# A Fourier transform, a mixture of experts and a rational layer on one core: odd frequencies from two half sums, a wider feature transform, and a rearranged hand-over

## Chip, cores, metric

One core of a Trainium2 chip. The metric is device microseconds (us) from start to end of one launch, less is better. The kernel before takes 3660.11 us, the median of three runs from 3656.12 to 3660.86.

## The reference, cut to what matters

```python
X = np.fft.fft(x, axis=1)          # x: (8, 3072, 256), float32
X = np.fft.fft(X, axis=2)
x = X.real.reshape(24576, 256)
logits = x @ w_gate                # 8 experts, one per token
expert = np.argmax(logits, 1)
gate = softmax(logits)[expert]
h = np.maximum(x[e] @ w1[e], 0)    # for the tokens of expert e: 256 -> 1024 -> 256
out = gate * (h @ w2[e])
h = out @ w_in                     # 256 -> 2048
g = (a0 + a1*h + a2*h**2 + a3*h**3) / (1 + |b0||h| + |b1|h**2 + 1e-6)
return g @ w_out                   # 2048 -> 256
```

## The kernel before, in words

**Two parts.** The first part (lines 226 to 928) computes the transform, chooses experts and writes each token's row into a DRAM buffer `xs`, sorted by expert. The second part (from line 933) runs the experts over 103 blocks of 256 sorted tokens and the rational layer over 96 blocks of tokens. The change lies in the first part and in the hand-over to the second.

**Steps.** The first part runs 16 steps, two for each of 8 batches (`jh` 0 and 1, half of the frequencies each), and a 17th that only finishes. `tc.manual_schedule()` is on: each engine runs its instructions in the order in which the code emits them, and so does SP, which issues nearly all DMAs on one queue. The main loop (lines 711 to 816) is thus the hand-written order. Work of three steps is interleaved in it: the sequence transform of step s, the feature transform of step s-1, the sorting and writing out of step s-2.

- *Folds* (`fold_a`, `fold_b`, `fold_c`, lines 302 to 343), on DVE: rows and columns that share a cosine or sine up to sign are added and subtracted, for the next batch. `ee` holds what the even frequencies need, `oo` what the odd ones need.
- *Sequence transform* (`stage1`, line 428), on PE in float32: for each step four sums, i = 0 and 1 over 3 chunks of 128 rows (even frequencies), i = 2 and 3 over 6 chunks (odd ones), 384 frequencies wide, so 18 matmuls. ACT moves each from PSUM into a tile `u`, with a correction row as a bias (`evac`).
- *Feature transform* (`stage2`, line 445; `second`, line 634): three groups g = 0, 1, 2 of a step, each for two sets of 128 frequencies. A set takes three matmuls of 137 columns, one of them only 8 rows deep (`u128`, the contribution of feature 128, through `rb`). ACT copies one half to SBUF (`pp`), and six DVE operations form sums and differences: rows `y` for a frequency and its mirror, and logits `L`. A group with g = 1 uses both even and odd `u`.
- *Choice and place* (`gate_a`, `gate_rank`, `gate_b`, lines 472 to 541): DVE and small f16 matmuls give each token its slot; `norms` (line 491) squares all 12 row sets of a step on ACT.
- *Scatter* (line 550): twelve indirect DMAs on POOL for a step, 128 rows each, into `xs`.
- *Weights' split* (`job_*`, lines 564 to 610): one 1 MB weight matrix for a step. SP loads it, ACT squares it into a sum (`job_square`, last on ACT in a step), a matmul with ones sums over partitions (in `gate_rank`), DVE makes a power of two (`job_factor`), ACT scales it in place and copies it to f16 (`job_scale`, `job_split`), POOL subtracts for the low half (line 605), SP stores 1 MB to `ws` at the head of the next step, behind the load of the next matrix. Two buffers each.

**Hand-over** (lines 818 to 1009, 1291 to 1309). The last step's tokens are sorted in two portions. ACT's queue writes eight zero blocks (line 839); DVE computes the block tables; SP reads an expert number and loads the first two blocks' weights into `wslot` (`gather_first`), then the first token blocks (`load`, line 1052). `words` decodes the float64 weights `w_in` on DVE in 12 portions, part of them in the last step and the rest at line 913. Then come the scale `sx`, `pairs` and `transp`, and the first expert matmul (line 1092).

Tables for the transform lie in the two `wslot` buffers until the weights need them.

## Time and profile before

| quantity | value |
|---|---|
| median of three runs | 3660.11 us |
| the profiled execution's own time | 3654.46 us |
| its span in the profile | 3652.7 us |
| mean granted TensorE clock | 0.974 of full |

All rows below are from the one profiled execution. A float32 matmul shows as two records in them. Busy time of an engine within a stretch is the union of its instructions; "idle before" names what ended a wait.

### The profile page before, as it was taken

Reading aid. Unit: us, or ns where it says so; the run is one execution under the profiler, and the core shown is the slowest. Engines: PE = TensorE matmul, PEld = TensorE weight load, DVE = VectorE, ACT = ScalarE, POOL = GpSimd, SP = SyncE. Lnnn points to the kernel's source line nnn. Section 1 sums busy time; section 2 is a strip of 40 time slices with the busy share of each in tenths; the row PEclk is TensorE's granted clock in tenths of the full one; section 3 lists DMA queues with packets and bytes.
Section 4 is the critical chain, followed back from the end, with each engine's and each line's share of the span. In section 5 each row is a group of like instructions: output and inputs, shape, how many; then the busy total and the mean of one; then the engine's idle time right before and its main releaser. Section 6 shows DMA issues by size and latency. Waiting matters only on the chain.

```text
span 3652.7 us, 76237 instructions
## 1 busy us (share of the span) xinstructions
PE 3490.5 (96%) x30238; PEld 3020.3 (83%) x30238; DVE 3126.7 (86%) x3629; ACT 3166.4 (87%) x3985; POOL 2899.8 (79%) x2569
## 2 busy tenths in 40 slices
PE   6999568999999999999999999999999999999997
PEld 3655357888888888888888888888888888888885
DVE  6888674898888888889888888889888888888987
ACT  3666445999999999999999999999999999999997
POOL 3777655888888888888888888888888888888876
PEclk9989689999999999999999999999999999999998
DMA  6665531322222121322231112221231112212110
GB/s 258 212 231 197 197 113 39 88 44 45 45 62 66 43 43 43 91 42 45 45 85 45 42 45 65 68 43 43 68 68 42 42 42 75 57 45 43 43 33 18
DMA packets 342823, 270.17 MB, mean 74 GB/s; under 512 B 180382, under 2 KB 317606, under 8 KB 335152
## 3 DMA queue, kind: packets, MB, share of 16 engines
q1 hardware_dynamic: 309184, 183.21, 21.1%
q0 software_dynamic: 33024, 79.96, 6.4%
q8 instruction: 237, 3.88, 0.6%
q10 hardware_dynamic: 256, 2.11, 0.2%
q14 instruction: 122, 1.00, 0.2%
HBM read 329.07 MB, written 96.92 MB: 117 GB/s over the span
## 4 chain that ended last, share of the span: by engine, by line
PE 88%; DVE 5%; issue 3%; ACT 2%; DMA 1%; another core or an unknown queue 0%; POOL 0%; ACTq 0%; POOLq 0%; DVEq 0%; SPq 0%
PE po L1252 27%; PE h L1092 14%; PE h L1093 14%; PE h L1095 14%; PE py L1095 5%; PE py L1092 5%; PE py L1093 5%; PE ps L437 3%; PE pq L456 1%; PE pq L454 1%; ACT sq L495 0%; PE pq L453 0%; PE pu L422 0%; DVE h L1230 0%
## 5 line engine op out<-in xcount | busy, mean ns | idle before, releaser
L1092 PE MATMUL h<-yr,win 128*128 128x256 f16 x3072 | 757.6, 274 | 8.0 <-DMA yr<-ys 4.6
L1093 PE MATMUL h<-yr,win 128*128 128x256 f16 x3072 | 757.5, 274 | 0.0
L1252 PE MATMUL po<-wout,ghi 128*128 128x256 f16 x6144 | 735.5, 273 | 10.8 <-ACT ghi L1239 7.6
L1252 PEld LDWEIGHTS <-ghi 128*128 128x128 f16 x6144 | 594.2, 98 | 81.2 <-ACT ghi L1239 12.2
L1095 PE MATMUL h<-yr,win 128*128 128x256 f16 x3072 | 588.7, 273 | 0.0
L1228 ACT ACTIVATE h<-L,bnd 128x1024 f32<-128x1024 f32 x385 | 429.6, 1116 | 19.9 <-DVE u__48655 L1219 1.5
L1092 PE MATMUL h<-xt,wslot 128*128 128x256 f16 x1648 | 406.7, 274 | 4.3 <-DVE hlo L1118 3.5
L1093 PE MATMUL h<-xt,wslot 128*128 128x256 f16 x1648 | 406.7, 274 | 0.0
L1252 PE MATMUL po<-wout,glo 128*128 128x256 f16 x3072 | 398.8, 273 | 2.2 <-POOL glo L1240 2.2
L1092 PE MATMUL py<-hhi,wslot 128*128 128x256 f16 x1648 | 374.2, 274 | 2.6 <-ACT hhi L1112 2.6
L1093 PE MATMUL py<-hhi,wslot 128*128 128x256 f16 x1648 | 374.2, 274 | 0.0
L1093 PEld LDWEIGHTS <-wslot 128*128 128x128 f16 x3296 | 324.0, 98 | 46.4 <-issue 7.9
L1095 PEld LDWEIGHTS <-wslot 128*128 128x128 f16 x3296 | 324.0, 98 | 42.1 <-issue 3.4
L1092 PEld LDWEIGHTS <-wslot 128*128 128x128 f16 x3296 | 324.0, 98 | 38.7
L1092 PEld LDWEIGHTS <-win 128*128 128x128 f16 x3072 | 301.6, 98 | 44.8 <-DMA yr<-ys 4.9
L1252 PEld LDWEIGHTS <-glo 128*128 128x128 bf16 x3072 | 300.4, 98 | 38.5 <-POOL glo L1240 3.6
L1095 PEld LDWEIGHTS <-win 128*128 128x128 f16 x3072 | 301.7, 98 | 35.8
L1093 PEld LDWEIGHTS <-win 128*128 128x128 f16 x3072 | 301.6, 98 | 35.7
L1095 PE MATMUL h<-xt,wslot 128*128 128x256 f16 x1648 | 316.1, 274 | 0.0
L552 POOL DMA_INDIRECT xs<-y,sli x192 | 215.2, 1121 | 91.5 <-issue 49.6
L1118 DVE SCALAR_TENSOR_TENSOR hlo<-h,hhi 128x1024 f16<-128x1024 f32 x197 | 239.7, 1217 | 23.9 <-ACT hhi L1112 17.4
L1265 POOL DMA_INDIRECT out_dram<-o,id x192 | 198.8, 1036 | 55.0 <-issue 46.5
(4935 smaller groups left out, 9499.9 us busy)
## 6 DMA issues: line engine op xcount, KB each, us to landing
xr<-xs SPq DMA_DIRECT2D x103, 258.0 KB
ys<-yw SPq DMA_DIRECT2D x103, 256.0 KB
yr<-ys SPq DMA_DIRECT2D x96, 256.0 KB
xh<-x_l SPq DMA_DIRECT2D x14, 1536.0 KB
wf<-in_moe_w_dram SPq DMA_DIRECT2D x16, 1024.0 KB
ws<-wh SPq DMA_DIRECT2D x16, 1024.0 KB
wslot<-ws SPq DMA_DIRECT2D x4, 1024.0 KB
xh<-x_l SPq DMA_DIRECT2D x4, 768.0 KB
```

What stands on the lines that cost most here:

```text
L437: nc.tensor.matmul(ps[0:m, 0:n], lhsT=lhsT, rhs=mat[:, c, 0:n], start=c == 0, stop=c == nk - 1)
L454: nc.tensor.matmul(pq[:, k, 0:137], lhsT=u128[0:B, par, jg:jg + 128], rhs=rb[0:B], start=False, stop=True)
L456: nc.tensor.matmul(pq[:, k, 256:393], lhsT=uou[0:P - 1, js], rhs=rs[0:P - 1], start=True, stop=True)
L552: ins = nc.gpsimd.indirect_dma_start(out=xs, out_offset=bass.IndirectOffsetOnAxis(ap=sli[:, t0 + t:t0 + t + 1], axis=0), in_=y[:, t], in_o ...
L1092: nc.tensor.matmul(ps, lhsT=wa[i], rhs=xa[i], start=i == 0, stop=False)
L1093: nc.tensor.matmul(ps, lhsT=wb[i], rhs=xa[i], start=False, stop=False)
L1095: nc.tensor.matmul(ps, lhsT=wa[i], rhs=xb[i], start=False, stop=i == n - 1)
L1118: V.scalar_tensor_tensor(out=hlo[:, sl], in0=ps, scalar=0.0, in1=hhi[:, sl], op0=ALU.max, op1=ALU.subtract)
L1228: nc.scalar.activation(out=ps, in_=L, func=AF.Exp, scale=-1.0, bias=st["bnd", j][3])
L1252: nc.tensor.matmul(ps[:, q], lhsT=g[:, f - fs[0], q * P:(q + 1) * P], rhs=wout[:, h, 4 * u + f], start=g is ghi and u == 0 and f == 0 and ...
L1265: ins = nc.gpsimd.indirect_dma_start(out=out, out_offset=bass.IndirectOffsetOnAxis(ap=t[:, q:q + 1], axis=0), in_=o[:, q], in_offset=None, ...
```

## The change

- Rows are dealt to chunks by parity, so that the sum of an odd frequency f over even rows and that over odd rows serve both f and its mirror 1536 - f. `stage1_odd` computes both sums for 384 frequencies over 3 chunks each; ACT moves one, and DVE's `parts` adds and subtracts the other. It runs twice for a batch: i = 2 late in a step with `jh` 0, i = 3 at the head of the step with `jh` 1. One table `co` and one `so` remain of two each.
- Feature 128's row becomes row 127 of the odd `u` tile, brought there by a DMA on SP's queue from `u128` (1.5 KB, from one partition to one): one for each `stage1` with i = 1, two in `parts` for i = 3. With it the feature transform takes two matmuls of 273 columns into the finished rows; ACT makes two copies of 512 elements out of PSUM, and DVE copies the logits.
- `norms` squares half of the row sets. The sum of a weight matrix is taken later in the step. `job_hi` scales and rounds in one ACT operation; `job_lo` forms the low half on DVE.
- `fold_c` writes `oo` in three pieces instead of one.
- Hand-over: `words` runs in the 15th and 16th steps, all 12 portions; the first block's weights are loaded in the 16th step, as expert 0's (every expert counts at least one block); the zero blocks go through SP; the scale's logarithm and the first `split_scale` come earlier.

```diff
+        tabs["co"] = carve(0, 6 * NH).rearrange("p (c j) -> p c j", c=6)
+        tabs["so"] = carve(1, 6 * NH).rearrange("p (c j) -> p c j", c=6)
         for i in range(2):
-            tabs[f"co{i}"] = carve(i, 6 * NH).rearrange("p (c j) -> p c j", c=6)
...
+        NC = D + 1 + 2 * E
+        rc, rs = carve(1, NC), carve(1, NC)
...
-                en.tensor_tensor(out=eo[2 + k][:, 3 * h:3 * h + 3], in0=f[:, 0], in1=f[:, 1], op=minus)
+                oo = eo[2 + k]
+                en.tensor_tensor(out=oo[:, h::3], in0=f[:, 0, 0::2], in1=f[:, 1, 0::2], op=minus)
+                for q in range(2):
+                    r = slice(64 * q, 64 * q + 64)
+                    en.tensor_tensor(out=oo[64 * h:64 * h + 64, 2 + 3 * q], in0=f[r, 0, 1], in1=f[r, 1, 1], op=minus)
...
+        def edge_col_odd():
+
+            pu = [psA.tile([P, 512], F32, tag="s1", name="pu") for _ in range(2)]
+            for q in range(2):
+                for i, c in enumerate((2 * q, 3 + 2 * q, 6 + q)):
+                    nc.tensor.matmul(pu[q][0:B, 0:NH], lhsT=xc[:, 3, c], rhs=tabs["co"][:, 3 * q + i],
+                                     start=i == 0, stop=i == 2)
...
+            if i == 1:
+                nc.sync.dma_start(out=ut[127:128], in_=u128[b:b + 1, 0, jh * NH:jh * NH + NH])
+            U[2 * b + jh][i] = ut
...
+        def stage1_odd(b, eo, i):
+
+            mat = tabs[("co", "so")[i - 2]]
+            m = 130 - i if i == 2 else P - 1
+            ps = [psA.tile([P, 512], F32, tag="s1", name="ps2") for _ in range(2)]
+            for q in range(2):
+                for c in range(3 * q, 3 * q + 3):
+                    nc.tensor.matmul(ps[q][0:m, 0:NH], lhsT=eo[i][:, c], rhs=mat[:, c], start=c == 3 * q,
+                                     stop=c == 3 * q + 2)
+            up, um = [p2.tile([P, NH], F32, tag=f"u{i}{q}", name=f"u{i}{q}") for q in range(2)]
+            evac(um[0:m], ps[0][0:m, 0:NH], ODD[i], [fb[0:m, i, s_, b:b + 1] for s_ in range(2)])
+            U[2 * b][i], U[2 * b + 1][i] = up, um
+
+            def parts():
+                a, o = um[0:m], ps[1][0:m, 0:NH]
+                V.tensor_tensor(out=up[0:m], in0=a, in1=o, op=ALU.add)
+                if i == 2:
+                    V.tensor_tensor(out=a, in0=a, in1=o, op=ALU.subtract)
+                else:
+                    V.tensor_tensor(out=a, in0=o, in1=a, op=ALU.subtract)
+                    for q, t in enumerate((up, um)):
+                        nc.sync.dma_start(out=t[127:128], in_=u128[b:b + 1, 1, q * NH:q * NH + NH])
+
+            return parts
...
-                nc.tensor.matmul(pq[:, k, 0:137], lhsT=ueu[:, js], rhs=rc, start=True, stop=False)
-                nc.tensor.matmul(pq[:, k, 0:137], lhsT=u128[0:B, par, jg:jg + 128], rhs=rb[0:B],
-                                 start=False, stop=True)
-                nc.tensor.matmul(pq[:, k, 256:393], lhsT=uou[0:P - 1, js], rhs=rs[0:P - 1],
-                                 start=True, stop=True)
-            pp = gp.tile([P, 2, 137], F32, tag="pp", name="pp")
-            nc.scalar.activation(out=pp, in_=pq[:, :, 0:137], func=AF.Copy)
-            La, Lm = L[:, 4 * g:4 * g + 2], L[:, 4 * g + 2:4 * g + 4]
-            ya, ym = y[:, 0:2], y[:, 2:4]
-            V.tensor_tensor(out=La, in0=pp[:, :, 129:137], in1=pq[:, :, 385:393], op=ALU.subtract)
-            V.tensor_tensor(out=Lm, in0=pp[:, :, 129:137], in1=pq[:, :, 385:393], op=ALU.add)
-            V.tensor_tensor(out=ya[:, :, 0:129], in0=pp[:, :, 0:129], in1=pq[:, :, 256:385], op=ALU.subtract)
-            V.tensor_tensor(out=ym[:, :, 0:129], in0=pp[:, :, 0:129], in1=pq[:, :, 256:385], op=ALU.add)
-            V.tensor_tensor(out=ya[:, :, 255:128:-1], in0=pp[:, :, 1:128], in1=pq[:, :, 257:384], op=ALU.add)
-            V.tensor_tensor(out=ym[:, :, 255:128:-1], in0=pp[:, :, 1:128], in1=pq[:, :, 257:384], op=ALU.subtract)
+                nc.tensor.matmul(pq[:, k, 0:NC], lhsT=u[2 * par][:, js], rhs=rc, start=True, stop=False)
+                nc.tensor.matmul(pq[:, k, 0:NC], lhsT=u[2 * par + 1][:, js], rhs=rs, start=False, stop=True)
+            nc.scalar.activation(out=y[:, 0:2, 0:D], in_=pq[:, :, 0:D], func=AF.Copy)
+            V.tensor_copy(out=L[:, 4 * g:4 * g + 4].rearrange("p (t k) e -> p t k e", t=2),
+                          in_=pq[:, :, D + 1:NC].rearrange("p k (t e) -> p t k e", t=2))
+            nc.scalar.activation(out=y[:, 2:4, 0:D], in_=pq[:, :, D:0:-1], func=AF.Copy)
...
-        def job_scale(n):
+        def job_hi(n):
             e, which = jobs[n]
-            wf = J[n][0]
-            nc.scalar.activation(out=wf, in_=wf, func=AF.Copy, scale=(s1c, s2c)[which][:, e:e + 1])
-
-        def job_split(n, engine=nc.gpsimd):
             wf, wh, _ = J[n]
-            nc.scalar.activation(out=wh[:, 0], in_=wf, func=AF.Copy)
-            engine.tensor_tensor(out=wh[:, 1], in0=wf, in1=wh[:, 0], op=ALU.subtract)
+            nc.scalar.activation(out=wh[:, 0], in_=wf, func=AF.Copy, scale=(s1c, s2c)[which][:, e:e + 1])
+
+        def job_lo(n):
+            e, which = jobs[n]
+            wf, wh, _ = J[n]
+            V.scalar_tensor_tensor(out=wh[:, 1], in0=wf, scalar=(s1c, s2c)[which][:, e:e + 1], in1=wh[:, 0],
+                                   op0=ALU.mult, op1=ALU.subtract)
...
+                Y[s] = p2.tile([P, 12, DX], F32, tag="y", name="y", bufs=3)
...
+            norms(Y[s][:, 4 * g:4 * g + 2], NQ[s][:, 2 * g:2 * g + 2])
...
-                yield from decode(raw_in[q % 3], win32[q], mq_in[:, q:q + 1])
-                if q == 0:
-                    load_words(3, raw_in[0])
+                yield from decode(raw_in[q % 2 if q < 2 else 0], win32[q], mq_in[:, q:q + 1])
+                if q in (0, 2):
+                    load_words(2 + q // 2, raw_in[0])
...
+        load_t("so")
...
-        load_t("co1")
+        load_t("se1")
         if B > 1:
             load_x(1, 1)
-        load_t("so1")
...
-                raw_in.append(wp.tile([P, 2048], F32, tag="wf", name="raw_c")
-                              .rearrange("p (f w) -> p f w", w=2).bitcast(I32))
-                load_words(2, raw_in[2])
+                for h in range(2):
+                    c = slice(4096 * h, 4096 * h + 4096)
+                    nc.sync.dma_start(out=wslot[0][:, c], in_=ws[0:P, c])
             if on:
                 b, jh = steps[s]
-                if jh == 0 and fold:
-                    nxt = new_eo()
-                u = U[s] = {}
-                if s and jh == 0:
-                    batch_row(b)
-                stage1(b, jh, eo, 0, u)
+                if jh == 0:
+                    if fold:
+                        nxt = new_eo()
+                    U[s], U[s + 1] = {}, {}
+                    stage1(b, 0, eo, 0)
+                else:
+                    parts = stage1_odd(b, eo, 3)
             if s == 0:
-                stage1(b, jh, eo, 2, u)
+                odd0 = stage1_odd(b, eo, 2)
                 job_square(0)
                 edge_logits()
-                batch_row(0)
+                odd0()
             if 2 <= s < NS:
                 second_norm(s - 2, 2)
             if fold:
                 fold_a(b + 1, jh)
+            if parts:
+                parts()
...
+                pr = gate_rank(s - 2, 12)
+                send(*finish(s - 2))
...
-                stage1(b, jh, eo, 1, u)
+                stage1(b, jh, eo, 1 - jh)
...
+            if s == NS - 2:
+                words(3)
...
+                    job_sum(n, pr[:, 144:145], start=False, skip_group_check=True)
+                    job_factor(n, pr[:, 144:145])
+                job_hi(n)
...
-                stage1(b, jh, eo, 2 if s else 1, u)
+                if s and jh == 0:
+                    parts = stage1_odd(b, eo, 2)
+                else:
+                    stage1(b, jh, eo, 1)
             if fold:
                 fold_c(b + 1, jh, nxt)
+            if parts:
+                parts()
...
-                job_split(n, nc.gpsimd if s != NS - 2 else V)
-            if on:
-                stage1(b, jh, eo, 3, u)
+                job_lo(n)
+            if s == NS - 2:
+                words(3)
...
-            v = nc.scalar.value_load(runi[0:1, e:e + 1], min_val=e * R, max_val=e * R + NT)
-            ins_z.append(nc.scalar.dma_start(out=xs[ds(v, TB), :], in_=cst["c_z"]))
+            v = nc.sync.value_load(runi[0:1, e:e + 1], min_val=e * R, max_val=e * R + NT)
+            ins_z.append(nc.sync.dma_start(out=xs[ds(v, TB), :], in_=cst["c_z"]))
...
-        for h in range(2):
-            gather_first(0, h)
...
+        V.tensor_scalar(out=nx2, in0=nx2, scalar1=1e-14, scalar2=None, op0=ALU.max)
+        nc.scalar.activation(out=nx1, in_=nx2, func=AF.Ln)
+        nc.scalar.activation(out=nx1, in_=nx1, func=AF.Exp, scale=-0.5)
...
-    pairs(0, 0)
-    pairs(0, 1)
...
+    step(3)
+    pairs(0, 0)
+    pairs(0, 1)
```

## Rows read from the trace of the kernel before

**Rows 1.** Page: span, PE's total, two groups of part 5.
```profile
span 3652.7 us, 76237 instructions
...
PE 3490.5 (96%) x30238; PEld 3020.3 (83%) x30238; DVE 3126.7 (86%) x3629; ACT 3166.4 (87%) x3985; POOL 2899.8 (79%) x2569
...
L552 POOL DMA_INDIRECT xs<-y,sli x192 | 215.2, 1121 | 91.5 <-issue 49.6
L1118 DVE SCALAR_TENSOR_TENSOR hlo<-h,hhi 128x1024 f16<-128x1024 f32 x197 | 239.7, 1217 | 23.9 <-ACT hhi L1112 17.4
```

**Rows 2.** Stretches: busy us of PE, PEld, DVE, ACT, POOL; PEclk, DMA share, GB/s.
```profile
28.64:78.01 49.37, 46.67 (x161) 25.04 (x162) 24.84 (x62) 23.16 (x48) 4.08 (x1) 0.97 0.61 225
78.01:97.14 19.13, 19.13 (x99) 12.71 (x98) 18.70 (x53) 15.12 (x41) 11.22 (x6) 1.00 0.46 148
78.01:352.20 274.19, 257.24 (x1195) 167.05 (x1194) 238.58 (x679) 183.62 (x478) 209.41 (x152) 0.91 0.65 217
398.45:473.88 75.43, 20.65 (x112) 13.96 (x111) 54.40 (x166) 19.98 (x61) 35.12 (x30) 0.56 0.51 173
```

**Rows 3.** PE in order of time: start, length, line, tiles, shape, records.
```profile
82.13 0.46 PE L503 MATMUL pr<-o,tri 128*128 128x88 f16 x11
...
83.02 2.18 PE L437 MATMUL ps<-se,ee 128*127 128x384 f32 x6
...
87.22 4.04 PE L437 MATMUL ps<-wslot,oo 128*128 128x384 f32 x12
91.09 0.40 PE L453 MATMUL pq<-wslot,u 128*128 128x137 f32 x2
...
473.88 0.37 PE L1092 MATMUL h<-xt,wslot 128*128 128x256 f16 x1 [0.78 <-DVE xt L1082]
```

**Rows 4.** DVE in order of time, two stretches.
```profile
211.13 0.17 DVE L462 TENSOR_TENSOR L<-pp,pq 128x16 f32<-128x16 f32 x1
...
212.62 0.25 DVE L476 TENSOR_REDUCE mx<-L 128x12 f32<-128x96 f32 x1
...
214.49 1.73 DVE L315 TENSOR_TENSOR fo<-xh 128x1524 f32<-128x1524 f32 x1
...
221.58 4.07 DVE L525 TENSOR_TENSOR pos<-pos,o 128x96 f32<-128x96 f32 x1
...
375.58 2.29 DVE L605 TENSOR_TENSOR wh<-wf,wh 128x2048 f16<-128x2048 f32 x1 [0.85 <-DMA xh<-in_moe_w_in_dram]
```

**Rows 5.** POOL in order of time; in brackets idle time and its releaser.
```profile
214.48 2.59 POOL L552 DMA_INDIRECT xs<-y,sli  x1 [0.30 <-issue]
...
221.43 4.09 POOL L605 TENSOR_TENSOR wh<-wf,wh 128x2048 f16<-128x2048 f32 x1
227.46 0.99 POOL L552 DMA_INDIRECT xs<-y,sli  x1 [1.94 <-DVE y L540]
...
375.73 3.00 POOL L552 DMA_INDIRECT xs<-y,sli  x1 [0.30 <-issue]
...
436.56 0.97 POOL L552 DMA_INDIRECT xs<-y,sli  x1 [6.22 <-DVE mx L476]
...
451.75 1.89 POOL L552 DMA_INDIRECT xs<-y,sli  x1 [0.30 <-issue]
```

**Rows 6.** SP (DMA issues) in order of time, two stretches.
```profile
201.79 0.38 SPq L569 DMA_DIRECT2D wf<-in_moe_w_dram  x1
202.22 0.46 SPq L609 DMA_DIRECT2D ws<-wh  x1
...
461.34 1.59 SPq L1052 DMA_DIRECT2D xr<-xs  x2
```

**Rows 7.** ACT in order of time, two stretches.
```profile
213.96 1.91 ACT L579 ACTIVATE wh<-wf 128x2048 f16<-128x2048 f32 x1 [2.05 <-issue]
...
432.57 0.40 ACT L459 ACTIVATE pp<-pq 128x274 f32<-128x274 f32 x1 [12.06 <-remote]
```

**Rows 8.** Chain of waits, first piece: start, length, what.
```profile
0.74 1.90 DMA pro<-x_r
```

274 lines of the change are left out of this document (131 added, 143 removed).

## Prediction

> **What bounds it now.** I read the stretches first, then the engines in order of time within one step. The second part of the kernel is PE at full clock and is left alone; the change must earn its time before 473.88 [rows 3]. The long piece there is the twelve steps from 78.01 to 352.20: 274.19 us, so 22.85 a step [rows 2]. PE is busy 257.24 of them, 94%, but at a granted clock of 0.91; the one step at clock 1.00, from 78.01 to 97.14, takes 19.13. So PE alone would need 19.13 / 0.91 = 21.0, and something else sets 22.85. POOL does: a scatter is 1.121 on the mean [rows 1] plus 0.30 between two [rows 5], twelve of them 17.05; then the subtraction of line 605, 4.09; then an idle 1.94 until DVE's `gate_b` has the next slots [rows 5]. The round is 23.1, the period within 1%. The reader is to see how it locks itself: DVE's line 525, in `gate_b`, lasts 4.07 and ends at 225.65 [rows 4], just after POOL's subtraction, which runs from 221.43 to 225.52. An operation of the same 96 elements takes 0.25 [rows 4]. DVE stands still for 3.8 us behind POOL, and POOL then waits for DVE. DVE is busy 238.58 / 12 = 19.9 a step, ACT 15.3, the DMA engines 0.65 x 22.85 = 14.9 [rows 2].
>
> **PE.** Six matmuls of 384 columns take 3.87 [rows 3], 0.645 each. Before: 18 x 0.645 = 11.6, ranks and sum 0.89 [rows 3], so 6.63 of the 19.13 for three feature groups, 2.2 each. After: 12 x 0.645 = 7.74; twelve matmuls of 273 columns at 273/384 of 0.645, 5.5 (1.84 a group); 0.89. Sum 14.1, or 15.5 at clock 0.91: 5.0 less at full clock, and off the bound if POOL or DVE keeps a longer round.
>
> **POOL.** The subtraction and its wait go; 17.05 of scatters stay. The new risk is `job_lo`: when DVE did one such subtraction (375.58, 2.29 long [rows 4]), the scatter begun at 375.73 lasted 3.00, against 0.99 and 0.97 at 227.46 and 436.56 [rows 5]; so did another lengthen, to 2.59 at 214.48, beside line 315's 1.73 [rows 4, 5]. The rounded ends are 0 and +2.0 a step, 17.05 to 19.1. I take 2.0: same data, same size, though `job_lo` is another operation. The Trainium skill (SBUF — State Buffer, "Who interferes with whom") says that a DVE instruction with two SBUF inputs contends with a GpSimd instruction that reads SBUF; by it the round is 19.1, without it 17.05, and the 3.00 agrees.
>
> **DVE.** Out go three groups' sums and differences, 1.49 each (211.13 to 212.62 [rows 4]), 4.5, and the collisions with line 605, up to 3.8. In come three logit copies at 0.17 as line 462 [rows 4], 0.5; `parts`, two operations of 384 elements, priced by line 1118 (1.217 for 1024 [rows 1]) at 0.46 each, 0.9; four more pieces in `fold_c`, 0.25 each at most, 1.0; `job_lo`, 2 x 1.217 = 2.4. From 19.9 that gives 20.2 less 0 to 3.8: 16.4 to 20.2. I take 17.6, since most steps collide. ACT gains six copies of 512 elements, a quarter of line 579's 1.91 [rows 7] plus overhead, 0.6 each, 3.6, and loses one pass of 2048, 1.9, and half the norms: at most 17.0, not the bound. DMA bytes hardly change.
>
> **The new wait.** In a step with `jh` 1 the second feature group reads the odd tile of i = 3, whose row 127 comes by a DMA that SP issues behind that step's weight load and store. Those two wait for `job_lo` of the step before, DVE's last act there: after PE's last group one logit copy 0.17, `gate_a` 1.9 (212.62 to 214.49 [rows 4]), `job_lo` 2.4, so 4.5 after PE has begun the new step; with two issues (0.43 and 0.46 [rows 6]) the rows leave at 5.4. No row shows a 1.5 KB transfer behind 2 MB. Ends: 1.9, as 32 KB took on an empty queue [rows 8], and 11.7, from the store's issue at 202.22 [rows 6] to 213.96, when `job_square`, which waits for load and store, began [rows 7]. I take 11.7: same queue, right behind the same transfers. So they land at 17.1 (at least 7.3). PE wants them after i = 3 (3.87), group 0 (1.84), the ranks (0.6) and i = 0 (1.94): 8.25, at clock 0.91 9.1. PE waits 8.0, and then has group 1, the sum, i = 1 and group 2, 5.9 or 6.5 at 0.91. That step takes 9.1 + 8.0 + 6.5 = 23.6; one with `jh` 0, where nothing fetched is read within the step, 15.5; the pair 39.1, **19.6 a step**. Behind PE in these 8 us wait ACT's copies, DVE's last logit copy, `gate_a` and `job_lo`, and so the next load: the wait feeds itself once a batch. POOL at 19.1 and DVE at 17.6 fit beneath. [...]
>
> **Twelve steps:** 12 x (22.85 - 19.6) = 39 less.
>
> **First two steps,** 28.64 to 78.01, 49.37 with PE busy 46.67 [rows 2]. Eighteen matmuls go (six in the first, twelve in the second, the edge columns included): 11.6 at most; nothing, if the second step already waits for its rows behind the first matrix's store. I take 6. Two tables less to load speak for more, but PE has no wait for them to lose.
>
> **15th and 16th steps.** All twelve decode portions now lie here, where folds are absent on DVE; the last one needs a load into a buffer that the previous portion frees, 1.9 to 11.7 of waiting on DVE, with the last slots behind it. Moving `job_lo` to DVE adds, dropping the sums takes away. I take 0, ends 6 better and 6 worse.
>
> **Hand-over.** ACT waited 12.06 at 432.57 to write `pp` [rows 7]; POOL then stood 6.22 before the last portion's scatters [rows 5]. `pp` is gone and a whole step's row tile was freed a step earlier: 6.2, at least 0. The last scatter ended at 451.75 + 1.89 = 453.64 [rows 5]; with 1.9 to land, 455.5, but the token load left at 461.34 [rows 6], behind the decodes: 5.8, at least 0. From there 12.5 passed to the first expert matmul [rows 3]; with the scale ready, I estimate 7.5 for load, split and transposes: 5, at least 0. Sum 17. The zero blocks on SP cost nothing while POOL still issues the last twelve scatters, 12 x 1.28 = 15 us: two issues with a register take 1.59 [rows 6], eight 6.4. Weights of block 0 come earlier and are off the path; the earlier `split_scale` hides behind the token load.
>
> **Sum.** 39 + 6 + 0 + 17 = 62. The profiled execution has a span of 3652.7 [rows 1] and its own time of 3654.46; less 62, **3592 us**. That execution is 5.6 below the median of the runs, which I leave within the range. About 0.2% is what a measurement of this kernel can tell from no change.
>
> **Rivals.** *Rows in time* (27%): the small DMAs land in 1.9 and `job_lo` does not stretch scatters. Then POOL at 17.05 and DVE at 17.6 set about 17.5: 12 x 5.35 = 64, start 11.6, tail 17, together 93: 3562. For it: their bytes are nothing. Against: the queue's order. *DMA in the way* (13%): 14.9 of DMA work a step is 76% of 19.6; the two weight transfers stretch from 11.7, ACT waits at `job_square`, PE at the sum. At 22 a step: 10 + 0 + 17 = 27: 3627. For it: the DMA share is 0.65 already. Against: a quarter of the DMA engines' time would still be free. *PE's clock falls* (6%), the slower side: PE, less busy, is granted the lower level of 1.2 GHz through the steps. Then its 14.1 take 28.3, longer than everything else: 12 x 5.4 = 65 more, less the tail's 17, 48 slower: 3702. For it: from 398.45 to 473.88 PE was busy 27% and its clock 0.56 [rows 2]. Against: PE would still be busy some 80%, nearer to the 94% that had 0.91. It decides where the clock falls below 14.1 / (22.85 + 17/12) = 0.58. *No gain* (4%): the 15th and 16th steps give back the tail's 17 and the rounds stay near 22: within 0.2%.
>
> **Numbers.** My forecast has 50%. Faster by over 0.2%: 0.50 + 0.27 + 0.13 and a little of the rest, 0.91; same 0.03; slower 0.06. The range: the low end is the first rival's 3562, less 6 for the 15th and 16th steps, 5 for steps at POOL's 17.05 and 6 for a shorter hand-over, 3545; the high end takes in the second rival's 3627, with 6 for those two steps and 3 for the hand-over, 3636.
>
> **What would show it.** Right: steps alternate, long with `jh` 1, PE idle before the second group until a DMA into `u`; scatters back to back on POOL, some near 3 us beside `job_lo`; line 525's successor at 0.25; first expert matmul some 62 earlier. Wrong: even steps of 17 to 18 with no such wait; ACT waiting for `ws` at `job_square`; a clock under 0.6 in the steps; DVE standing at a decode while POOL is idle in the 16th step.

## The result, and the profile after

The changed kernel takes 3627.52 us (median of four runs, 3622.71 to 3630.88) where the kernel before takes 3659.82 (3656.12 to 3660.86) on the same chip: ratio 0.9913, 95% interval 0.9895 to 0.993, 32 us less. The forecast, 3592, is 62 below the kernel before's profiled execution of 3654.46. The profiled execution has its own time of 3622.71 and a span of 3620.9.

The top of the page, to be held against [rows 1]: PE has 88 us less work, DVE 35, ACT 54, POOL 57, and the span is 32 shorter. What came off the engines did not all come off the time.

```profile
span 3620.9 us, 75124 instructions
...
PE 3402.7 (94%) x29842; PEld 2967.4 (82%) x29842; DVE 3091.3 (85%) x3424; ACT 3111.9 (86%) x3791; POOL 2842.4 (78%) x2558
```

To compare stages I need the same places in both. A pair of steps (one batch) begins with the six even matmuls of 385 columns. By these, the 3rd step of the kernel before begins at 78.01 and its 15th at 347.86; the 352.20 at which [rows 2] cut the stretch is 4.3 us into the 15th. The stretches of busy time (columns as in [rows 2]), first of the kernel before, cut there:

```profile
78.01:347.86 269.85, 252.90 (x1178) 164.21 (x1176) 234.28 (x665) 182.10 (x475) 206.06 (x148) 0.91 0.65 215
```

and of the changed kernel: first two steps, twelve steps, 15th and 16th to the first scatter of the 15th step's tokens, and from there to the first expert matmul.

```profile
29.32:74.17 44.85, 37.33 (x112) 19.68 (x113) 25.27 (x51) 16.91 (x31) 0.00 (x0) 0.92 0.46 166
74.17:323.83 249.66, 195.19 (x889) 130.04 (x887) 202.75 (x526) 142.63 (x329) 165.93 (x139) 0.87 0.74 243
323.83:398.64 74.81, 39.72 (x185) 25.59 (x185) 49.57 (x121) 32.64 (x75) 32.09 (x30) 0.76 0.53 191
398.64:449.62 50.98, 9.62 (x61) 6.37 (x60) 26.42 (x107) 7.83 (x24) 27.35 (x27) 0.60 0.45 141
```

| stage | before | after | gained | forecast |
|---|---|---|---|---|
| first two steps | 49.37 | 44.85, begun 0.7 later | 3.8 | 6 |
| twelve steps | 269.85 | 249.66 | 20.2 | 39 |
| 15th and 16th steps | 66.09 | 74.81 | -8.7 | 0 |
| hand-over | 59.93 | 50.98 | 8.9 | 17 |
| second part | 3178.8 | 3171.3 | 7.5 | 0 |

In the twelve steps no engine is full: PE 195 of 250 us at a granted clock of 0.87, DVE 203, POOL 166, the DMA engines 0.74. PE's list of waits in them (waited for: total, times, longest) has one large entry under two names. The wait is the same in all six batches; where the profile found no event for it, it says "issue".

```profile
PE pq L499 <- issue: 22.9, 3, 8.1
PE pq L499 <- DMA u<-u: 21.0, 3, 8.0
PE pr L544 <- issue: 4.1, 7, 0.9
PE pr L539 <- DVE o L522: 2.7, 3, 1.2
```

One step with `jh` 1, PE in order of time (216.20 to 241.23), then SP in the same step:

```profile
216.20 4.03 PE L474 MATMUL ps<-wslot,oo 128*127 128x384 f32 x12
...
222.57 2.18 PE L457 MATMUL ps<-wslot,ee 128*128 128x384 f32 x6
...
234.15 1.25 PE L499 MATMUL pq<-wslot,u 128*128 128x273 f32 x2 [8.01 <-issue]
...
235.48 4.07 PE L457 MATMUL ps<-se,ee 128*127 128x384 f32 x6
```

```profile
222.82 0.38 SPq L605 DMA_DIRECT2D wf<-in_moe_w_dram  x1
223.25 0.46 SPq L646 DMA_DIRECT2D ws<-wh  x1
223.76 1.17 SPq L488 DMA_DIRECT2D u<-u  x2
```

SP issues the 1 MB weight load, the 1 MB store and then the rows of 1.5 KB; PE goes on 10.4 us after the rows' issue began (10.1 to 10.5 in the six batches). Ahead of the load SP stood 6.1 us for `job_lo` of the step before (line 641), so the rows leave 7.6 us into the step. A row moves as 16 packets of 96 bytes; these start at 231.47, when those of the store are nearly out, the last one of the two rows ends some 8.7 us after the issue began, and the DMA engines are busy all that time. SP's wait, and the stretch from the issue on:

```profile
SPq L605 <- DVE wh L641: 6.1, 1, 6.1
```

```profile
223.76:232.69 8.93, 2.38 (x10) 1.38 (x8) 6.05 (x18) 1.89 (x6) 6.95 (x7) 0.80 1.00 326
235.48:239.55 4.07, 4.07 (x8) 2.33 (x9) 3.37 (x10) 2.96 (x7) 3.16 (x3) 0.53 0.21 76
```

Behind the wait stands a second cost: the six matmuls at 235.48 take 4.07, six of the same size at 222.57 take 2.18. PE had stood still for 8 us; in the 4 us of these matmuls its granted clock is 0.53 (second row), nearly all of it at the lower of its two levels (1.2 GHz), and they run at about half pace.

DVE and POOL, for the rounds of [rows 4, 5]: line 558, the successor of line 525, takes 0.25 where that took 4.07, and POOL has no subtraction, but the scatter that runs beside `job_lo` (line 641) lengthens.

```profile
203.79 2.34 DVE L641 SCALAR_TENSOR_TENSOR wh<-wf,s2c,wh 128x2048 f16<-128x2048 f32 x1
...
209.96 0.25 DVE L558 TENSOR_TENSOR pos<-pos,o 128x96 f32<-128x96 f32 x1
```

```profile
202.84 1.01 POOL L588 DMA_INDIRECT xs<-y,sli  x1 [0.30 <-ACT y L503]
204.16 2.83 POOL L588 DMA_INDIRECT xs<-y,sli  x1 [0.30 <-issue]
212.71 1.65 POOL L588 DMA_INDIRECT xs<-y,sli  x1 [5.72 <-issue]
```

In the 15th step the loads of `w_in`'s words, issued on SP at 332.50 behind 2 MB of weights, hold DVE at the first decode until 345.45. ACT's part of that decode stands ahead of its copies, so PE waits 9.61 next, and POOL runs dry for 17.05 (at 369.28) and 12.66 (at 398.64).

```profile
345.45 0.80 DVE L223 TENSOR_SCALAR xh<-xh 128x1024 int32<-128x1024 int32 x1 [7.36 <-issue]
```

```profile
354.70 1.65 PE L474 MATMUL ps<-wslot,oo 128*127 128x384 f32 x2 [9.61 <-ACT u L421]
```

In the hand-over POOL is no longer late (its longest idle is 2.20, against 6.22 in [rows 5]). But the last scatter ends at 433.4 and the first token load leaves at 442.98: the eight zero blocks on SP, which wait for DVE's counts, are issued from 423.09 to 440.02, and the load's last wait is for one of them to land. SP's waits (waited for: total, times, longest) and SP in order of time:

```profile
SPq L1096 <- DMA xs<-c_z: 1.6, 2, 1.4
```

```profile
423.09 16.93 SPq L878 DMA_DIRECT2D xs<-c_z  x8
442.98 1.64 SPq L1096 DMA_DIRECT2D xr<-xs  x2
```

### The profile page after: what moved, and what is told of

The parts are those of the page before. It is cut to its first block, busy times and chain, and to the rows that moved or that the text cites. A ratio compares the mean times of both kernels' runs of the same rounds, so it can differ in the third digit from the quotient of the medians.

```text
span 3620.9 us, 75124 instructions
## 1 busy us (share of the span) xinstructions
PE 3402.7 (94%) x29842; PEld 2967.4 (82%) x29842; DVE 3091.3 (85%) x3424; ACT 3111.9 (86%) x3791; POOL 2842.4 (78%) x2558
## 4 chain that ended last, share of the span: by engine, by line
PE 84%; DVE 7%; issue 3%; DMA 3%; ACT 2%; POOL 1%; SPq 0%; another core or an unknown queue 0%; POOLq 0%; DVEq 0%; ACTq 0%
PE po L1296 27%; PE h L1136 14%; PE h L1137 14%; PE h L1139 14%; PE py L1139 5%; PE py L1136 5%; PE py L1137 5%; PE ps L457 1%; DMA u<-u 1%; PE ps L474 1%; DMA xh<-in_moe_w_in_dram 0%; DVE wh L641 0%; PE pq L499 0%; DVE oo L352 0%; DVE h L1274 0%
## 5 line engine op out<-in xcount | busy, mean ns | idle before, releaser
L588 POOL DMA_INDIRECT xs<-y,sli x192 | 222.6, 1159 | 181.0 <-issue 102.8
```

The lines of the kernel that those rows point to most:

```text
L588: ins = nc.gpsimd.indirect_dma_start(out=xs, out_offset=bass.IndirectOffsetOnAxis(ap=sli[:, t0 + t:t0 + t + 1], axis=0), in_=y[:, t], in_o ...
```

## The experiments

Twelve kernels ran, in three groups of four, each group on one chip beside the kernel before (the second and the third group on the same chip). That kernel took 3642.4, 3645.5 and 3661.8 us in the three groups, so kernels are compared by their ratio to it, and stages only roughly across groups. The table is read like the one above; the clock is that granted to PE in the twelve steps.

| kernel | ratio to before (95%) | first two | a step | clock | 15th, 16th | hand-over |
|---|---|---|---|---|---|---|
| before, profiled first | 1 | 49.4 | 22.49 | 0.91 | 66.1 | 59.9 |
| changed, profiled first | 0.9913 (0.9895, 0.993) | 44.9 | 20.81 | 0.87 | 74.8 | 51.0 |
| changed, again | 0.9921 (0.9905, 0.9938) | 45.7 | 21.00 | 0.88 | 73.1 | 42.3 |
| rows on ACT's queue | 0.9844 (0.9827, 0.986) | 38.2 | 18.82 | 0.92 | 75.7 | 42.5 |
| rows early | 0.9827 (0.981, 0.9843) | 46.2 | 17.73 | 0.98 | 76.1 | 42.1 |
| weights after rows | 0.9799 (0.9775, 0.9823) | 39.0 | 18.42 | 0.95 | 70.6 | 48.6 |
| words first | 0.99 (0.9884, 0.9917) | 45.8 | 20.85 | 0.89 | 63.6 | 42.1 |
| rows and words | 0.9772 (0.9756, 0.9789) | 40.8 | 17.74 | 0.98 | 60.2 | 42.1 |
| before, with the new split | 0.9884 (0.9867, 0.99) | 50.2 | 19.40 | 0.99 | 51.6 | 56.0 |
| changed, with the old split | 1.0101 (1.0079, 1.0122) | 46.8 | 25.90 | 0.82 | 80.4 | 56.6 |

**Rows on ACT's queue.** The same transfers, issued by another engine.

```diff
-                nc.sync.dma_start(out=ut[127:128], in_=u128[b:b + 1, 0, jh * NH:jh * NH + NH])
+                nc.scalar.dma_start(out=ut[127:128], in_=u128[b:b + 1, 0, jh * NH:jh * NH + NH])
...
-                        nc.sync.dma_start(out=t[127:128], in_=u128[b:b + 1, 1, q * NH:q * NH + NH])
+                        nc.scalar.dma_start(out=t[127:128], in_=u128[b:b + 1, 1, q * NH:q * NH + NH])
```

> All the row transfers into the odd tiles are issued on ACT's queue instead of SP's, at the same place of the program. Theory (ring order: in the changed kernel PE's 8 us before the second feature group of each step with jh 1 is a 1.5 KB row standing behind the 2 MB that SP issued just before it): the row lands some 2 us after its issue, the 6.4 to 8.1 us idle of PE before line 499 goes, those steps fall from 25.0 to 17 to 18 us, and the kernel is 40 to 55 us shorter than the changed one, near 3575 to 3587. Rival 1 (the DMA engines are full with 2 MB whatever queue a transfer is in): the row lands as late as before, PE's idle stays, 3620 to 3630. Rival 2 (the wait is hidden behind another bound, DVE or POOL with the stretched scatters): PE's wait goes, but the steps fall by 2 to 3 us only, 3605 to 3615.

It gained some 27 us (0.9844 against 0.9917, the mean of the two runs of the changed kernel), about half of what the theory said. The trace shows why. SP issues the weights at 204.32 and 204.75; ACT issues the first row at 205.00, as soon behind the store as SP did; PE goes on at 212.30, 7.3 us after the issue began (6.5 to 7.3 in the six batches), not 10.4 and not 2. ACT's first issue and PE's wait in order of time, then PE's waits at this line in the twelve steps:

```profile
205.00 0.50 ACTq L488 DMA_DIRECT2D u<-u  x1
```

```profile
212.30 1.25 PE L499 MATMUL pq<-wslot,u 128*128 128x273 f32 x2 [4.69 <-DMA u<-u]
```

```profile
PE pq L499 <- DMA u<-u: 18.5, 5, 4.8
PE pq L499 <- DVE nrm L584: 8.6, 2, 4.5
```

So the place in SP's queue is worth 3 us of the 10.4. On a queue of its own the row's first packet still starts only 4.9 us after its issue (205.00) and the last ends after 7.0, where two rows with no other issue of SP in the 12 us before them (those of the first batch in the run of rows and words below, issued at 46.94) were through after 2.1. Theory and first rival each hold a part; whether it is the work of the DMA engines or the making of the packets that holds the row for the 4.9, no run separates. PE's wait at line 499 in the twelve steps is 27.1 us in all (the 8.6 put down to DVE are the wait of two batches at the same place), against 51.3 in the changed kernel run again.

**Rows early.** The two rows of the odd tiles go out at the start of the step before, ahead of that step's weights, from the second batch on.

```diff
-            up, um = [p2.tile([P, NH], F32, tag=f"u{i}{q}", name=f"u{i}{q}") for q in range(2)]
+            up, um = early.pop((b, i), None) or odd_tiles(i)
...
+            if on and s and s % 2 == 0:
+                early[steps[s][0], 3] = odd_tiles(3)
+                odd_rows(steps[s][0], early[steps[s][0], 3])
             for n in new:
                 job_load(n)
```

> The two rows of the odd tiles of i = 3 are fetched at the start of the step before, ahead of its weight load on SP, from the second batch on; nothing else changes queue. Theory (order on SP's queue is all that matters): the same gain as with the rows on ACT's queue within 5 us, but the wait in the first batch's second step stays. Rival (the row's own transfer through busy DMA engines is slow): also gone here, since there are 16 us more, while the run with ACT's queue keeps it; so the two runs differ by 40 us.

The wait for `u` is gone from PE's list, the clock is 0.98 and a step takes 17.73; the first batch keeps its wait (46.2 for the first two steps, against 38.2 with the rows on ACT's queue). The twelve steps fall by 39 us against the changed kernel run again, the kernel by 33 (0.9827 against 0.9917). The two runs differ by 6 us in all, near what the theory said, but only because the first batch's wait offsets the steps: there the early rows are 13 us better. From the second batch on they still take 6 to 9 us from the issue to the last packet, but leave 16 us or more before the step that reads them begins. The twelve steps, then PE's waits and POOL's scatters in them:

```profile
75.92:288.69 212.77, 182.31 (x889) 119.83 (x887) 201.70 (x525) 140.36 (x329) 160.05 (x133) 0.98 0.87 279
```

```profile
PE ps L457 <- DVE ee L355: 13.2, 5, 2.8
PE pr L628 <- DVE run L566: 9.2, 12, 1.6
PE pq L508 <- DVE u L491: 3.5, 5, 0.9
```

```profile
L597 POOL DMA_INDIRECT xs<-y,sli x133 | 160.0, 1203 | 98.2 <-DVE L L510 57.8 <-issue 29.7 <-DMA xs<-y,sli 2.7
```

All that PE still waits for is DVE, busy 201.70 of 212.77. But POOL is as full: 57.2 of the 98.2 us idle lie ahead of its first scatter, at 87.53, and from there on it has, but for one gap of 1.1, only the 0.30 between two scatters. Twelve of them take 18.0 (1.203 and 0.30 each), a little more than a step.

**Weights after rows.** The block of loads and stores is moved down in the step, with nothing else.

```diff
-            for n in new:
-                job_load(n)
-            for n in old:
-                job_store(n)
-            old = now
...
             if parts:
                 parts()
+            for n in new:
+                job_load(n)
+            for n in old:
+                job_store(n)
+            old = now
```

> In every step the weight load and store come after the rows of the odd tiles in the program, and so behind them on SP's queue; nothing else moves (w_in's words thereby also come ahead of the weights in the 15th step). Theory (the row waits for the 2 MB ahead of it and for nothing else): PE's wait before line 499 is gone in the first batch too, steps of 17.7 to 18.5 us, 15th step as with the words first; 35 to 45 us below the changed kernel, 0.980 to 0.983 of the kernel before. Rival (the weights, now some microseconds later, make ACT wait at the square and PE at its sum): PE's wait moves to the sum, steps of 19 to 20 us, 15 to 25 below the changed kernel.

0.9799, at the edge of what the theory said: the wait is gone in every batch, the first two steps take 39.0, a step 18.42. But the theory's reason is not what the trace shows. In the twelve steps the rows take little less time, 7.4 to 8.3 us from the issue to the last packet against 8 to 9 in the changed kernel; in all batches but the last 1.5 MB of `x` now stand just ahead of them. What changed is when they leave: in the step that begins at 119.97 after 0.4 us, and in no batch later than 0.9, where the changed kernel has 6.2 to 7.8. SP's wait for `job_lo` now comes behind them. SP in order of time:

```profile
120.00 0.33 SPq L278 DMA_DIRECT2D xh<-x_l  x1
120.39 1.13 SPq L488 DMA_DIRECT2D u<-u  x2
126.51 0.38 SPq L605 DMA_DIRECT2D wf<-in_moe_w_dram  x1
```

The pairs vary between 33.5 and 40.1, and a step is 0.7 longer than with the early rows. The rival's wait at the sum is not the reason: it is 7.8 us in all, 8.5 in the changed kernel run again. Of the 8.3 us over twelve steps 5.0 are busy time of PE (187.33 for 182.31, at a clock of 0.95 for 0.98); where the rest goes is open. Five lines moved (`w_in`'s words come ahead of the weights by it too) make the change worth 74 us by the ratio, instead of 30.

**The split alone.** The kernel before, with only the weights' split as in the changed kernel.

```diff
-            nc.scalar.activation(out=wf, in_=wf, func=AF.Copy, scale=(s1c, s2c)[which][:, e:e + 1])
+            nc.scalar.activation(out=J[n][1][:, 0], in_=wf, func=AF.Copy, scale=(s1c, s2c)[which][:, e:e + 1])
...
-            nc.scalar.activation(out=wh[:, 0], in_=wf, func=AF.Copy)
-            engine.tensor_tensor(out=wh[:, 1], in0=wf, in1=wh[:, 0], op=ALU.subtract)
+            V.scalar_tensor_tensor(out=wh[:, 1], in0=wf, scalar=(s1c, s2c)[which][:, e:e + 1], in1=wh[:, 0],
+                                   op0=ALU.mult, op1=ALU.subtract)
```

> The kernel before with the weights' split alone changed as in the changed kernel: the scaled high part in one ACT pass, the low part on DVE, nothing left on POOL but the scatters. Theory (POOL's subtraction of 4.1 us and DVE's 4.07 us operation beside it lock the round at 22.5 us): the lock opens and PE at its granted clock of 0.91 sets some 21 us a step, 12 to 18 us less in all. Rival 1 (PE was the bound all along): within 5 us of the kernel before. Rival 2 (the low part stretches scatters to 2.5 to 3 us and fills DVE, whose sums and differences are still there, 19.9 less 3.8 plus 2.4): no gain or some us slower.

This part alone gives 0.9884, 42 to 44 us, more than the whole change (0.9921 in the same group; the intervals, up to 0.99 and from 0.9905, do not overlap, and the medians are 15 us apart). The theory was right in kind and too low: a step takes 19.40, not 21. The row of the twelve steps says how; below it PE's two largest entries in the list of waits of the kernel before, same steps, and there one load (SP) and the square that waits for it (ACT):

```profile
78.48:311.24 232.76, 231.51 (x1178) 153.55 (x1177) 226.42 (x678) 161.20 (x462) 167.74 (x137) 0.99 0.76 254
```

```profile
PE pr L583 <- ACT wh L579: 5.8, 4, 2.4
PE pr L583 <- issue: 5.5, 3, 3.5
```

```profile
225.55 0.38 SPq L572 DMA_DIRECT2D wf<-in_moe_w_dram  x1
...
238.40 1.91 ACT L579 ACTIVATE wh<-wf 128x2048 f16<-128x2048 f32 x1 [4.63 <-DMA ws<-wh]
```

The same 1178 PE records are busy 231.51 us at a clock of 0.99, where the kernel before had 252.90 at 0.91. PE is now full, and without the stalls it keeps its clock. Of the 37 us that the steps fell, 21 are busy time that shrank with the clock and 16 are idle time. Of PE's 17 us idle in the kernel before, 11.3 were at the sum of the weights (line 583). There the subtraction reached PE: SP issued the next load, and the store behind it, as soon as POOL's subtraction had ended at 225.52 [rows 5], and ACT's square, which the sum needs, stood 4.63 us until that store had landed. The edit also drops one of ACT's passes of 1.9 us; no run separates that from the subtraction.

**The old split in the changed kernel.** The reverse: scaled in place and copied by ACT, subtracted on POOL.

```diff
-            nc.scalar.activation(out=wh[:, 0], in_=wf, func=AF.Copy, scale=(s1c, s2c)[which][:, e:e + 1])
+            nc.scalar.activation(out=wf, in_=wf, func=AF.Copy, scale=(s1c, s2c)[which][:, e:e + 1])
...
-            V.scalar_tensor_tensor(out=wh[:, 1], in0=wf, scalar=(s1c, s2c)[which][:, e:e + 1], in1=wh[:, 0],
-                                   op0=ALU.mult, op1=ALU.subtract)
+            nc.scalar.activation(out=wh[:, 0], in_=wf, func=AF.Copy)
+            engine.tensor_tensor(out=wh[:, 1], in0=wf, in1=wh[:, 0], op=ALU.subtract)
```

> The changed kernel with the weights' split where the kernel before had it: scaled in place by ACT, copied by ACT, subtracted on POOL. Theory (POOL's subtraction next to DVE's work locks the round whatever PE has to do): POOL needs 17.05 and 4.1 and its wait for the slots again, some 22.5 us a step instead of 21.0, the kernel 15 to 30 us over the changed one, near or above the kernel before. Rival (in the changed kernel the row that lands late sets the round once a batch, and POOL catches up within it): within 5 us of the changed kernel.

1.0101: slower than the kernel before, and 1.8% over the changed kernel, more than twice what the theory said. A step takes 25.90. The subtraction does not just lengthen POOL's round: the next weight load and the store wait for it (one runs from 263.20 to 267.27, and SP issues the load at 267.30), and the rows stand behind these on SP's queue. Stretch and PE's first wait in it:

```profile
76.75:387.51 310.76, 197.19 (x889) 129.19 (x888) 200.44 (x514) 164.03 (x342) 211.66 (x156) 0.82 0.59 197
```

```profile
PE pq L499 <- DMA u<-u: 96.9, 10, 17.1
```

The wait for the rows has nearly doubled (96.9 us against 51.3, up to 17.1 at once). So the new transform without the new split would have lost 1%.

**Words first.** In the 15th step the loads of `w_in`'s words are issued ahead of the weights.

```diff
+            if s == NS - 2:
+                for q in range(2):
+                    load_words(q, raw_in[q])
             for n in new:
                 job_load(n)
             for n in old:
                 job_store(n)
             old = now
-            if s == NS - 2:
-                for q in range(2):
-                    load_words(q, raw_in[q])
```

> In the 15th step the two loads of w_in's words stand ahead of the weight load and store on SP. Theory (DVE's 7.4 us at the first decode, and behind it ACT's 7.9 and PE's 9.6, come from words that land late behind 2 MB of weights): the words land some 5 to 8 us earlier, the 15th and 16th steps fall from 74.8 us to 66 to 70, the kernel is 5 to 9 us shorter. Rival (the decodes themselves, on DVE's path, fill the steps): DVE's wait goes but the two steps stay within 2 us of 74.8.

The words are issued 0.3 us before the step's first matmul instead of 8.7 after it; DVE's 7.4 us at the first decode is gone, PE's 9.6 behind it falls to 3.4, and the two steps take 63.6 instead of 73.1 to 74.8. The time falls by 5 to 8 us (0.99 against 0.9913 and 0.9921; the intervals overlap, so the stage shows it, not the total).

**Rows and words.** Early rows in the first batch too, words first, and a third buffer for the third portion.

```diff
-                yield from decode(raw_in[q % 2 if q < 2 else 0], win32[q], mq_in[:, q:q + 1])
-                if q in (0, 2):
-                    load_words(2 + q // 2, raw_in[0])
+                yield from decode(raw_in[q % 3], win32[q], mq_in[:, q:q + 1])
+                if q == 0:
+                    load_words(3, raw_in[0])
...
                 edge_col_odd()
+                early[0, 3] = odd_tiles(3)
+                odd_rows(0, early[0, 3])
```

> The rows of the odd tiles issued one step early in every batch, the first too; in the 15th step w_in's words ahead of the weights on SP; in the 16th a third buffer for the third portion, so that the fourth has nothing to wait for. Theory (the two waits are separate and add up): steps of 17.7 to 18 us as in the run with early rows, the second step without its 5 us wait, 15th and 16th steps of 58 to 64 us instead of 74.8; some 12 to 18 us under the run with early rows alone, 0.978 of the kernel before. Rival (once the steps are shorter DVE, then 95% busy, is late into the 15th step and takes back what the words gave): under 6 us below the run with early rows.

3560.38 us where the kernel before took 3645.47 and the changed one 3616.22: 0.9772. It beats both, by 85 and 56 us, and by its ratio it is 20 us under the run with early rows alone. The waits were separate and add up: 17.74 a step, 40.8 for the first two, 60.2 for the 15th and 16th. The third buffer, with all else that differs in these two steps, is worth 3.4 us at most (63.6 less 60.2).

**Twice the low part.** The kernel of the last run, with `job_lo` done twice a step.

```diff
             for n in now:
                 job_lo(n)
+                job_lo(n)
```

> The run with early rows and words, with the low part computed twice on DVE in every step (the second time over the first). Theory (with the rows in time DVE, busy 95% of the twelve steps, is the bound): each step is 2.3 us longer, 20.0 instead of 17.7, the kernel 27 to 36 us longer. Rival (POOL's scatters or the wait for weights set the round and DVE has slack behind them): under 15 us.

0.985 (0.983 to 0.987), 0.0078 or 28.5 us more, and 20.29 a step instead of 17.74: 2.55 more for an operation of 2.34 (steps of two groups). DVE has no slack once the rows are in time. By the run with early rows POOL has none either; here, with longer steps, POOL stands 0.8 to 1.9 us before the scatters of nearly every step.

**Zero blocks on ACT's queue.**

```diff
-            v = nc.sync.value_load(runi[0:1, e:e + 1], min_val=e * R, max_val=e * R + NT)
-            ins_z.append(nc.sync.dma_start(out=xs[ds(v, TB), :], in_=cst["c_z"]))
+            v = nc.scalar.value_load(runi[0:1, e:e + 1], min_val=e * R, max_val=e * R + NT)
+            ins_z.append(nc.scalar.dma_start(out=xs[ds(v, TB), :], in_=cst["c_z"]))
```

> The eight zero blocks go back to ACT's queue. Theory (the 16.9 us that SP spends on them delay the first token load, 442.98, past the last scatter's end at 433.4): the token load leaves 6 to 8 us earlier and the kernel is 6 to 8 us shorter, about 3620. Rival (the load waits for the decodes or for the last scatter's data to land, whichever queue the zeros use): less than 2 us. Second rival: ACT, which has the scale and the splits of the hand-over to do, is held by the issues instead, 0 to 5 us longer.

A miss. The token load left at 435.32, 1.9 after the last scatter's end at 433.46, as the theory wanted, but the ratio is 0.9928 (0.9911 to 0.9944), no better than the changed kernel.

**The changed kernel again**, unaltered.

> The changed kernel, unaltered, beside the others on one chip: the runs so far were compared with the kernel before alone, whose time differed by 17 us between two chips. If its ratio to the kernel before is 0.9913 here too, it stands near 3611 where the kernel before takes 3642; then the rows issued early were worth 30 us, the rows on ACT's queue 25, the words first 5, and the zero blocks on ACT cost 6. If instead the changed kernel keeps its 3627 on every chip and only the kernel before varies, they were worth 47, 41, 22 and 11.

The first case held, and it explains the miss: here the zero blocks are still on SP, and the load leaves at 435.98, 1.95 after the last scatter.

```profile
415.98 10.33 SPq L878 DMA_DIRECT2D xs<-c_z  x8
435.98 1.63 SPq L1096 DMA_DIRECT2D xr<-xs  x2
```

The zero blocks began 7 us earlier than in the first profile, because DVE's counts were ready, and their eight issues took 10.33 us, not 16.93. In the first profile ACT had stood still in the 16th step; below it PE's last matmuls of the line that it reads, and the same ACT instruction in the second profile:

```profile
412.92 0.60 ACT L500 ACTIVATE y<-pq 128x512 f32<-128x512 f32 x1 [8.68 <-remote]
```

```profile
405.94 0.63 PE L499 MATMUL pq<-wslot,u 128*128 128x273 f32 x2
```

```profile
408.04 0.60 ACT L500 ACTIVATE y<-pq 128x512 f32<-128x512 f32 x1 [2.33 <-PE pq L499]
```

It is the kind of wait that [rows 7] show with 12.06. The view names no engine for it, but in the trace the semaphore that ends it is one that only PE raises: it comes 6.3 us after the end that the profile gives the last matmul (406.57; these ends are modelled). ACT has such a wait, of 7.3 to 12.1 us, near the end of the steps in the profiles of the kernel before, of the changed kernel's first run and of all four runs of the third group (weights after rows, twice the low part, the old split, and the scales in one go), with PE's semaphore 3.4 to 6.7 us after that end in each, and none in the eight of the other two groups. Where it is seen the kernel before took 3660 to 3662, elsewhere 3642 to 3646. So it goes neither with a kernel nor with the chip, since the second and the third group share theirs; why PE's signal comes late stays open.

**The scale of `w_in` later**, after the first piece of the second part.

```diff
-    step(3)
     pairs(0, 0)
...
-        step(1)
+        step(1 if i else 4)
```

> In the changed kernel the scale of w_in's split is found after the first piece of the second part, about where the kernel before had it, not ahead of the first tokens' split. Theory (this move is where the second part's 7.5 us came from, 3178.8 against 3171.3 from the first expert matmul to the end): the second part is 5 to 8 us longer, the kernel 3 to 8 longer, since the hand-over gets shorter by at most a few. Rival (the 7.5 came from elsewhere in the second part, or is a difference of two chips): within 3 us of the changed kernel.

0.9928 (0.9911 to 0.9944), second part 3170.7 where the changed kernel again has 3171.9. The rival holds: its place is not where the second part gained.

**The scales in one go.** The pieces between a scale's reductions and matmuls are taken out as well.

```diff
         V.tensor_reduce(out=mq[:, 0:1], in_=mq, axis=AX.X, op=ALU.max)
-        yield
...
         V.tensor_reduce(out=m, in_=pt, axis=AX.X, op=ALU.max)
-        yield
```

> The changed kernel with each of its two scales of the second part found in one go again, no pieces of expert work between its reductions and matmuls, and the first one after the first piece, as in the kernel before. Theory (what the second part gained, 130 to 125 us from the first expert matmul to the first matmul with w_in's table, is PE's 2.5, 2.8 and 0.7 us at the two scales, which are now broken into three): that stretch takes 129.5 to 131 us again and PE's waits at the two transposes of the scale return, 2.5 to 3 us each. Rival (it came from the freer queues at the start of the second part, since the weights of block 0 are loaded earlier): the stretch stays at 124.5 to 126.

Between the two: 127.0 us from the first expert matmul to the first with `w_in`'s table, where the changed kernel has 124.9 and 123.2 and the kernel before 130.4. PE's wait at the second scale is back, 2.8; the first one fell where PE waited anyway. So the pieces explain 2 to 4 us of the 7.5; the rest is open.

```profile
PE topt L1021 <- DVE mq_out L1019: 2.8, 1, 2.8
PE topb L1024 <- DVE topm L1022: 0.7, 2, 0.4
```

## Why the prediction was half right

Of the 62 us 31.7 came. Missing are 18.8 in the twelve steps, 8.7 in the 15th and 16th, 8.1 in the hand-over and 2.2 at the start; 7.5 came unforeseen in the second part. The mechanism that was to set the steps, PE waiting for the rows, is there. The step of the prediction that failed most is "**19.6 a step**", the time of PE around that wait: it measured 20.81.

**The round of [rows 2 to 5]: right in kind, wrong in price.** POOL's subtraction did hold up the round; the weights' split alone gave 42 us. Wrong is "PE alone would need 19.13 / 0.91 = 21.0". The clock of 0.91 was taken as given, but it came with the very stalls that the change removes: with the split alone it is 0.99 and a step takes 19.40. The sum of 62 does not use the 21.0. But by it the forecast saw 1.9 us a step to be had from the lock (22.85 less 21.0) where 3.1 were (22.49 less 19.40), and did not see that the rest of the change had to beat 19.4, not 22.85. Against the split alone the change is 15 us slower. Nor does its account of the kernel before have the wait at the sum of the weights, by which the lock reached PE.

**The new wait: right.** It stands where it was put, before the second feature group of each step with `jh` 1, behind the weights on SP. Rows there at 17.1 us into the step: PE went on at 234.15 - 216.20 = 17.95. PE waiting 8.0: measured 6.4 to 8.1. Taking 11.7 for the transfer, and not 1.9, was the choice that decided the forecast, and it was nearly right: 10.4. That the wait came out to the tenth is partly luck: the rows left at 7.6 and not 5.4, and PE wanted them at 9.9 and not 9.1. The reason given, "same queue, right behind the same transfers", holds for 3 us, by the run on ACT's queue. The Trainium skill (DMA: Bandwidth & Descriptors, "Queues, rings and completion order") says that descriptors on each DMA engine are consumed in ring order; the packets of the rows, the first at 231.47 where the store's last starts at 231.98, agree. But with the rows ahead of the 2 MB the transfer is hardly shorter, and the wait is gone because they leave 7 us earlier.

**Twelve steps, 39 forecast, 20.2 measured: the term that was mis-sized.** 4.3 us of it was never there: the stretch of [rows 2] did not end at a step. The rest is a step of 20.81 instead of 19.6, 14.5 us over twelve. PE's busy time there is 195.19 where 12 x 15.5 = 186 was reckoned, since the clock is 0.87, not 0.91: the forecast let PE stand 8 us and then go on at the old clock, and the matmuls behind the wait ran at 4.07 for 2.18. PE's small waits, the other entries of its list, which the forecast put at nothing, add 10.4; the six waits for rows were 43.9, not 48. 9 + 10 - 4 = 15.

**15th and 16th steps, 0 forecast, 8.7 lost.** The forecast looked at the last portion's buffer; the loss came at the first one, whose words stand behind 2 MB on SP. It had priced just this queue for the rows and did not apply it to the words two lines further down. With the words first the two steps take 63.6.

**Hand-over, 17 forecast, 8.9 measured; 13.7 in the second profile** (42.3 against the 56.0 of the kernel before with the new split, in the same group). POOL's idle 6.2 went, and from load to first matmul 6.6 passed for 7.5. The step that failed is "`pp` is gone": the 12.06 of [rows 7] was not a wait for the buffer `pp` but for PE's signal. An 8.68 of the same kind came at its successor, DVE's counts came late with it, and through them the zero blocks, which the forecast had at 6.4 us on SP and out of the way. They took 16.93 and held the load for 7.6.

**First two steps, 6 forecast, 3.8 measured.** As feared there, the second step waits for its rows; with the wait gone they take 38.2 to 40.8.

**Second part, nothing forecast, 7.5 gained.** That the earlier scale "hides behind the token load" was true of its place and missed the breaking-up, which saves PE's wait of 2.8 at the second scale; the rest has no shown cause.

**The rivals.** "Rows in time" is not what happened, but its price was right: 17.5 a step for POOL and DVE, and 17.73 once the rows are early. There both engines are full, DVE at 95% and POOL with 18.0 for twelve scatters, where this rival had 17.05: a scatter beside `job_lo` takes 2.5 to 3.0, as forecast. The Trainium skill (SBUF — State Buffer, "Who interferes with whom") says that a DVE instruction with two SBUF inputs contends with a GpSimd instruction that reads SBUF; the 2.83 at 204.16 agrees. "DMA in the way" named 22 a step; at a DMA share of 0.87 the steps still run at 17.7. That its 3627 is the time measured is luck: PE waited for the rows and not at the sum. "PE's clock falls" did not decide, but a small part of it, 0.87, is in the miss. The range, 3545 to 3636, holds the result.

## What to carry to other kernels

A transfer of a few KB costs what stands ahead of it: before putting one into a step, see what its queue has to wait for before it can issue it and what the DMA engines carry just then, and issue it earlier if nothing forbids. When one part of a change opens a lock, time that part alone first: a change that is faster as a whole can hide a part that is slower. The granted clock of 0.91 in the stretch with stalls went up to 0.99 when the stalls went; reckon the stage after the change with the clock of a stretch that has none.

## What was not expected of the hardware

- 1.5 KB took 10.4 us behind 2 MB on the same queue and 7.3 on a queue of its own with the same 2 MB just issued, from the start of the issue to PE's going on. Issued ahead of the 2 MB but behind 1.5 MB of `x`, two such rows still took 7.4 to 8.3 us to their last packet; with no issue of SP in the 12 us before them, 2.1.
- The same 1178 PE records were busy 252.90 us at a granted clock of 0.91 and 231.51 at 0.99; after 8 us idle six matmuls took 4.07 at a granted clock of 0.53, where six of that size take 2.18.
- The kernel before took 3642 to 3646 us in two groups and 3660 to 3662 in two others; with the latter two goes a wait of 7 to 12 us on ACT, in all six of their profiles, for a semaphore of PE that comes 3.4 to 6.7 us after the end that the profile gives PE's last matmul.
